# A fused attention, maxout and softplus kernel on one core: the last two blocks of an output phase interleaved by tiles, and loads and preparations moved

## The chip, the core and the metric

The kernel runs on one core of a Trainium2 chip as one program. A core has five engines with one instruction queue each: TensorE (PE) multiplies matrices and writes PSUM; VectorE (DVE), ScalarE (ACT) and GpSimd (POOL) work element by element; SyncE (SP) issues most of the DMA transfers, and ACT issues some. The metric is the device time of one execution in microseconds (us); lower is better.

## The reference

```python
def sm_attn(qq, kk, vv):                       # per batch and head: 8 batches, 8 heads
    s = scale * np.matmul(qq, kk.transpose(0, 1, 3, 2))
    s = s - np.max(s, axis=-1, keepdims=True)
    a = np.exp(s)
    a = a / (np.sum(a, axis=-1, keepdims=True) + 1e-09)
    return np.matmul(a, vv)
p_packed = sm_attn(p, k, v)                    # p: 32 x 64, k and v: 576 x 64
out = sm_attn(q, p_packed, p_packed)           # q: 576 x 64
x = np.ascontiguousarray(attn_out.transpose(0, 2, 1, 3)).reshape(B * S, H * D)   # 4608 x 512
h = np.maximum(np.maximum(x @ w1, x @ w2), x @ w3)         # d_ff 768
x = (h @ w_out).astype(np.float32)
h = x @ w_in                                               # d_ff 2048
g = np.maximum(h, 0.0) + np.log1p(np.exp(-np.abs(h)))      # softplus
return (g @ w_out).astype(np.float32)
```

The weights arrive as 64-bit floats and are narrowed on the chip. Every float32 product is made of three products of rounded halves (hi x hi, hi x lo, lo x hi), so each operand is split into a hi part (a copy by ACT, L125) and a lo part (a subtraction by DVE or POOL, L127).

## The kernel before

The first part goes batch by batch, n = 0 to 7. A hand-written order opens it (batch 0 and what batch 1 needs); batches 1 to 7 are the loop `for n in range(1, B)`. A batch has ten slots. Slots 0 to 5 are the first layer of the first network: each slot has three units (u = 3 * slot + w), a unit is twelve matmuls of 288 columns (`three`, L481), and its PSUM result is copied by ACT for w = 0 (L508) and folded in by DVE with a maximum for w = 1 and 2 (L510, tile m). "m17" below is the DVE maximum of unit 17, the last one of a batch, "m4" that of unit 4. Slots 6 to 9 are the second layer (`layer2`), four times 36 matmuls. Between the units stands the attention of the batch after (`small_work`): its first scores at unit 5 (`scores1`, PE tile ps_s at L286, with transposed k), the transposed weights at units 9 to 12, the values at unit 13 (`values`, L357, with the tile vt), and its second scores directly behind unit 17 (`scores2`, also L286, with transposed q). The weights packed for the first layer are ps_w at L459.

q and k come in four loads of two heads each (g = 0 to 3, `load_raw`, L186), v in one load (`load_v`, L198, tile vt). DVE transposes each q and k load (L253, L256, tile vT). A score takes its heads in the order g = 0 to 3, twice over.

PE's order in this part is pinned (`pinned`), SP's too (`in_turn`). The order on DVE, ACT and POOL is not written down: a scheduler that models the times of instructions and of transfers decides it when the program is built, and on the chip each engine then executes its list in that order.

In the last batch the preparations of the second part stand in the table `BATCH_END`: loads, sums and splits of the first tokens (loadx, sumx, splitx) and of the first weight pairs (load, sum, split).

The second part is written out in order for PE, DVE, ACT and SP. It has five blocks of tokens, c = 0 to 4: four of 2 x 512 tokens and a short one of 2 x 256. For each of eight column pairs j, `layer3` makes seven products of six matmuls (L960, four PSUM buffers of tag l3), adds them up in the tile h (one buffer of tag h; ACT at L977, DVE at L975), and `finish` applies softplus (L998) and splits the result into ghi and glo (two buffers each). `layer4` multiplies these into four accumulators acc0 to acc3, one for each 128 tokens, three matmuls each (L1024, L1025, L1026); the third one needs glo. In the long blocks `second_half` does the same for the kept second halves. `store` copies an accumulator out (ACT for even tiles at L1031, DVE for odd ones at L1033) and issues four DMAs (L1038), in the short block two from SP and two from ACT.

Of the kernel before, what the change touches and what calls it, by code (L numbers as in the profile page):

```python
# [8 lines left out]
F32 = mybir.dt.float32  # L9
# [10 lines left out]
def packed_attention_maxout_softplus(  # L20
# [741 lines left out]
    def narrow_ahead():  # L762
# [19 lines left out]
        4: [("sumx", 2), ("splitx", 2), ("load", 0)],  # L782
        5: [("sumx", 3), ("splitx", 3), ("load", 1)],
        6: [("sum", 0), ("split", 0)],
        7: [("load", 2)],
        8: [("sum", 1), ("split", 1)],
        9: [("load", 3)],
    }

    for n in range(1, B):  # L790
        for slot in range(F1 + KC):
# [4 lines left out]
            if slot < F1:  # L796
                if slot == 1 and n + 1 < B:
                    in_turn(load_v, n + 1)
                for w in range(3):
                    small_work(n, 3 * slot + w)  # L800
                    pinned(layer1_unit, n, slot, w)
            else:
                small_work(n, 2 * F1 + slot)
                pinned(layer2, n, slot - F1)
# [3 lines left out]
            for at, ahead, g, which in loads:  # L808
                if at == slot and n + ahead < B:
                    in_turn(load_raw, n + ahead, g, which)  # L810
            store_narrowed()
            if 0 < n < B - 1 and slot < F1:
# [123 lines left out]

    w2t, kept, hs, gt, accs = {}, {}, {}, {}, {}
    NTT = CH // P
# [24 lines left out]
    def layer3(c, j, aside):  # L963


        def between(at):
            for fn, *args in aside.get(at, ()):
                fn(*args)

        w, wide = pairs.pop(j), BLOCKS[c][1]  # L970
        h = cp.tile([P, 7 * CH], F32, tag="h", name="h")
        h = hs[c, j] = h[:, : 7 * wide].rearrange("p (a t) -> p a t", a=7)

        def plus(o, a, ps):
            add(out=h[:, o], in0=h[:, a], in1=ps, op=ALU.add)  # L975

        nc.scalar.activation(out=h[:, 3], in_=product(c, w, 0, 0), func=AF.Copy)  # L977
        between(0)
        plus(0, 3, product(c, w, 1, 1))
        plus(4, 3, product(c, w, 4, 4))  # L980
        between(1)
        ps = product(c, w, 3, 3)
        plus(5, 4, ps)
        plus(6, 4, product(c, w, 5, 5))
        plus(3, 6, ps)
        between(2)
        plus(2, 6, product(c, w, 2, 6))
        plus(1, 5, product(c, w, 6, 2))
        between(3)

    def split_g(key, src):
        hi = gp.tile([P, CH], F32R, tag="ghi", name="ghi")
        lo = gp.tile([P, CH], F32R, tag="glo", name="glo")
        split(src, hi, lo)
        gt[key] = (hi, lo)

    def softplus(out, x):
        nc.scalar.activation(out=out, in_=x, func=AF.Softplus)  # L998

    def finish(c, j):  # L1000

        h = hs.pop((c, j))
        if BLOCKS[c][1] == CH:
            if j == 0:
                kept[c] = gsp.tile([P, F2, CH], F32, tag="gs", name="gs").rearrange(
                    "p (i j) t -> p i j t", i=2
                )
            softplus(h[:, 0:3:2], h[:, 0:3:2])
            softplus(kept[c][:, :, j], h[:, 1:4:2])
            mine = [h[:, 0], h[:, 2]]  # L1010
        else:
            softplus(h[:, 0:4], h[:, 0:4])
            mine = [h[:, 2 * i : 2 * i + 2].rearrange("p a t -> p (a t)") for i in range(2)]
        for i in range(2):
            split_g((c, j, i), mine[i])

    def layer4(c, half, f, tts, first, last):
        ghi, glo = gt[c, f % FP, f // FP]
        whi, wlo = w2t[f]
        for tt in tts:  # L1020
# [5 lines left out]
            nc.tensor.matmul(ps, glo[:, cols], whi, start=False, stop=last)  # L1026

    def store(c, half, tt, o):
        ps = accs.pop(tt)
        if tt % 2 == 0:  # L1030
            nc.scalar.activation(out=o, in_=ps, func=AF.Copy)  # L1031
# [17 lines left out]
    def second_half(c, aside):  # L1049
        order = [j + FP * i for j in range(FP) for i in range(2)]  # L1050

        def ready(f):
            split_g((c, f % FP, f // FP), kept[c][:, f // FP, f % FP])

        ready(order[0])
        store_first(c)
        for i, f in enumerate(order[:-1]):
# [3 lines left out]
            else:  # L1061
                for tt in range(NTT):
                    layer4(c, 1, f, [tt], False, False)
                    layer4(c, 1, order[-1], [tt], False, True)
            for fn, *args in aside.get(i, ()):
# [19 lines left out]
    with tc.manual_schedule(engines={E.PE, E.DVE, E.Activation, E.SP}):  # L1085
        for f in (0, FP, 1, 1 + FP):
            load_w2(f)
        for i, (c, j) in enumerate(seq):
            aside = {0: [], 1: [], 2: [], 3: []}
            if c == 0:  # L1090
                for m in {0: (), 1: (0,), 2: (1,), 3: (2, 3)}.get(j, (j,)):
# [10 lines left out]
            if c + 1 < NCH:  # L1102
                for part in range(2):
                    if j == (FP - 3 if c == 0 else 1) + part:
                        aside[3].append((load_x2, c + 1, part))
                    if j == FP - 1 and part == 0 or j == FP - 2 and part == 1 and c > 0:
                        aside[0].append((sum_x2, c + 1, part))
            layer3(c, j, aside)
            if i + 2 < len(seq):
                get_pair(*seq[i + 2])  # L1110
            halves = BLOCKS[c][1] == CH
            if j > 0:
                for a in range(2):
                    layer4(c, 0, j - 1 + FP * a, range(NTT), j == 1 and a == 0, False)
            finish(c, j)
            if j == FP - 1:
# [10 lines left out]
                else:  # L1127
                    for tt in range(NTT):
                        for a in range(2):
                            layer4(c, 0, j + FP * a, [tt], False, a == 1)  # L1130
                    store_first(c)
# [36 lines left out]
```

## Time and profile before

| what | us |
|---|---|
| median of 3 runs | 1255.85 (1255.2 to 1256.78) |
| the profiled execution, its own time | 1259.18 |
| its span, first to last instruction | 1257.3 |
| PE busy | 1238.8 (99%) |
| DVE busy | 687.2 (55%) |
| ACT busy | 463.3 (37%) |
| POOL busy | 117.6 (9%) |

The profiled execution took 3.3 us more than the median of the three runs; its own time holds 1.9 us outside its span. Matmuls are pipelined and their ends are modelled, so the distance between the starts of two matmuls says more than PE's busy share. A value in square brackets behind a row is the time that the engine stood idle before that row, and what ended the wait.

### The profile page before, as it was taken

What the parts mean: (1) busy time and instruction counts of PE and PEld (TensorE: products, weight loads), DVE (VectorE), ACT (ScalarE), POOL (GpSimd) and SP (SyncE); (2) the same over time, 40 slices, a digit from 0 to 9 for tenths busy, and PEclk for the clock granted to TensorE, in tenths of its full rate; (3) what the DMA queues carried; (4) which work ended last, traced back from release to release, by engine and by line L of the source; (5) the groups of instructions that cost most, each with busy time, mean ns of one, the idle gap of its engine ahead of it and who ended that gap; (6) DMA issues with size and microseconds to landing.
All of it is one profiled execution on the core that took longest, in us unless ns stands there. A gap on an engine that the chain in (4) does not pass through costs nothing.

```text
span 1257.3 us, 21088 instructions
## 1 busy us (share of the span) xinstructions
PE 1238.8 (99%) x8647; PEld 1060.9 (84%) x8647; DVE 687.2 (55%) x1070; ACT 463.3 (37%) x686; POOL 117.6 (9%) x112
## 2 busy tenths in 40 slices
PE   8899999999999999999999999999999999999998
PEld 6688989898989899888888888888888888888897
DVE  2975757565666649577564444634455354452443
ACT  3744343434343435344342222423224222232222
POOL 1432212222231201000000000000000000000000
PEclk8999999999999999999999999999999999999999
DMA  9878585869596612665523333315334143330541
GB/s 241 260 212 210 143 230 160 212 191 250 155 239 171 175 52 98 232 252 184 192 68 107 137 118 126 117 34 209 117 117 126 25 159 125 126 135 1 200 177 43
DMA packets 87008, 192.55 MB, mean 153 GB/s; under 512 B 12160, under 2 KB 56448, under 8 KB 81792
## 3 DMA queue, kind: packets, MB, share of 16 engines
q1 hardware_dynamic: 81920, 181.24, 47.9%
q10 hardware_dynamic: 4992, 9.96, 2.3%
q8 instruction: 68, 1.11, 0.4%
q14 instruction: 28, 0.23, 0.1%
HBM read 149.23 MB, written 41.94 MB: 152 GB/s over the span
## 4 chain that ended last, share of the span: by engine, by line
PE 92%; DMA 4%; DVE 2%; issue 1%; ACT 0%; SPq 0%; DVEq 0%; ACTq 0%
PE ps L481 28%; PE ps L960 27%; PE acc L1026 11%; PE acc L1025 10%; PE acc L1024 10%; PE ps_w L459 2%; DMA qraw<-in_q_dram 2%; PE ps_s L286 1%; DMA vt<-in_v_dram 1%; PE ps_v L357 1%; PE ps_e L330 1%; DVE x2lo L127 1%; DVE xu L833 0%; DMA praw<-in_p_dram 0%; DVE m L510 0%
## 5 line engine op out<-in xcount | busy, mean ns | idle before, releaser
L960 PE MATMUL ps<-x2hi,wc 128*128 128x512 f32 (+1 forms) x1120 | 322.9, 369 | 1.2 <-ACT h L977 1.2
L975 DVE TENSOR_TENSOR h<-h,ps 128x512 f32<-128x512 f32 (+1 forms) x280 | 173.8, 633 | 114.4 <-PE ps L960 104.5
L960 PEld LDWEIGHTS ps<-x2hi,wc 128*128 128x128 f32 x1120 | 203.6, 188 | 37.2 <-ACT h L977 1.4
L1026 PE MATMUL acc<-w2hi,glo 128*128 128x512 f32 x576 | 225.4, 391 | 0.0
L1025 PE MATMUL acc<-w2lo,ghi 128*128 128x512 f32 x576 | 224.8, 390 | 0.0
L1024 PE MATMUL acc<-w2hi,ghi 128*128 128x512 f32 x576 | 224.5, 390 | 0.0
L960 PE MATMUL ps<-x2lo,wc 128*128 128x512 f32 (+1 forms) x560 | 206.4, 369 | 0.0
L127 DVE TENSOR_TENSOR glo<-h,ghi 128x512 fp32r<-128x512 f32 x80 | 54.8, 692 | 159.9 <-ACT ghi L125 159.9
L1026 PEld LDWEIGHTS acc<-w2hi,glo 128*128 128x128 f32 x576 | 108.1, 188 | 24.6 <-DVE glo L127 2.1
L1024 PEld LDWEIGHTS acc<-w2hi,ghi 128*128 128x128 f32 x576 | 108.2, 188 | 23.7 <-ACT ghi L125 1.2
L998 ACT ACTIVATE h<-h 128x1024 f32<-128x1024 f32 x40 | 42.4, 1060 | 232.0 <-DVE h L975 232.0
L481 PE MATMUL ps<-a2hi,pwhi 128*128 128x288 f32 x576 | 127.8, 303 | 0.0
L1025 PEld LDWEIGHTS acc<-w2lo,ghi 128*128 128x128 f32 x576 | 108.1, 188 | 22.9
L481 PE MATMUL ps<-a2hi,pwlo 128*128 128x288 f32 x576 | 123.2, 295 | 0.4 <-DVE pwlo L127 0.4
L481 PE MATMUL ps<-a2lo,pwhi 128*128 128x288 f32 x576 | 123.3, 296 | 0.0
L960 PEld LDWEIGHTS ps<-x2lo,wc 128*128 128x128 f32 x560 | 105.5, 188 | 18.4
L481 PEld LDWEIGHTS ps<-a2hi,pwhi 128*128 128x128 f32 x576 | 91.8, 189 | 15.1 <-ACT m L508 5.0
L510 DVE TENSOR_TENSOR m<-ps,m 128x576 f32<-128x576 f32 x96 | 72.4, 754 | 49.9 <-PE ps L481 45.1
L481 PEld LDWEIGHTS ps<-a2hi,pwlo 128*128 128x128 f32 x576 | 92.7, 189 | 0.7 <-DVE pwlo L127 0.7
L481 PEld LDWEIGHTS ps<-a2lo,pwhi 128*128 128x128 f32 x576 | 92.8, 189 | 0.0
L127 DVE TENSOR_TENSOR pwlo<-ps_w,pwhi 128x1024 fp32r<-128x1024 f32 (+1 forms) x40 | 44.5, 1114 | 84.0 <-ACT pwhi L125 83.9
L127 DVE TENSOR_TENSOR glo<-gs,ghi 128x512 fp32r<-128x512 f32 x64 | 44.1, 690 | 78.7 <-ACT ghi L125 70.6
(103 smaller groups left out, 1486.7 us busy)
## 6 DMA issues: line engine op xcount, KB each, us to landing
wc<-wic SPq DMA_DIRECT2D x32, 1792.0 KB
qraw<-in_q_dram SPq DMA_DIRECT2D x112, 140.0 KB
wic<-wc SPq DMA_DIRECT2D x8, 1792.0 KB
kraw<-in_k_dram SPq DMA_DIRECT2D x96, 140.0 KB
vt<-in_v_dram SPq DMA_DIRECT2D x8, 1152.0 KB
wraw<-in_moe_w_dram SPq DMA_DIRECT2D x18, 512.0 KB
x2d<-xs ACTq DMA_DIRECT2D x32, 288.0 KB
xu<-x2d SPq DMA_DIRECT2D x72, 128.0 KB
```

What stands on the lines that cost most here:

```text
L127: engine.tensor_tensor(out=lo, in0=src, in1=hi.bitcast(F32), op=ALU.subtract)
L286: nc.tensor.matmul(ps[G][cols, hh, :HS], w[rows, cols], x[rows, g, hh * HS : hh * HS + HS], start=True, stop=True,)
L330: nc.tensor.transpose(ps[: 32 * TI, i // hi, (i % hi) * P : (i % hi) * P + P], e[:, i], ident,)
L459: nc.tensor.matmul(ps[cols, G, : units * P].rearrange("p (w x) -> p w x", w=units), ppT[n][rows, cols], wsb[rows, 4 * c : 4 * c + units, g ...
L481: nc.tensor.matmul(o, w, xx, start=first, stop=last)
L510: nc.vector.tensor_tensor(out=m, in0=ps[:, :, :HS], in1=ms[n, f], op=ALU.max)
L960: nc.tensor.matmul(out, l, r, start=(i == 0), stop=(i == len(terms) - 1))
L975: add(out=h[:, o], in0=h[:, a], in1=ps, op=ALU.add)
L998: nc.scalar.activation(out=out, in_=x, func=AF.Softplus)
L1024: nc.tensor.matmul(ps, ghi[:, cols], whi, start=first, stop=False)
L1025: nc.tensor.matmul(ps, ghi[:, cols], wlo, start=False, stop=False)
L1026: nc.tensor.matmul(ps, glo[:, cols], whi, start=False, stop=last)
```

## The change

- `last_two` replaces the order of the last two blocks f of an output phase. Before, each tile tt took its three matmuls of the first block and then its three of the second. Now the first block goes over tiles 0, 1 and 2, then the second over 0 and 1, then the first over 3, then the second over 2 and 3. It is used at the end of `second_half` and at the end of the short block.
- In the short block two pairs j share one tile h, each in its half, in place of a new tile each; and the softplus and the splits of pair 0 are issued in three steps between the products of pair 1.
- The last tile of the whole kernel is copied out in two halves, one by ACT and one by DVE.
- `load_v` of the next batch moves from the start of slot 1 to slot 0, behind the first of the three q loads there. SP then issues v ahead of the q loads g = 1 and 2.
- In `BATCH_END` sumx 3, splitx 3 and load 1 go from slot 5 to slot 6, sum 0 and split 0 to slot 7, split 1 to slot 9.

What these do to the order on the engines is shown at three places. First, DVE at the end of the first layer in batch 3. In the names, vT_3162 is the transposed q of batch 4, qraw_3164 its last load (g = 3), m_3426 to m_3507 the maxima of units 13, 14, 16 and 17, x32 the narrowing of later weights, s2 the second scores. Before:

```order
L510 TENSOR_TENSOR m_3426<-ps_1_3413,m_3338 128x576
L510 TENSOR_TENSOR m_3441<-ps_1_3428,m_3426 128x576
L253 STREAM_TRANSPOSE vT_3162<-qraw_3164 128x576
L111 SCALAR_TENSOR_TENSOR x32_3315<-x32_3315,raw64_3068 128x512
L510 TENSOR_TENSOR m_3492<-ps_1_3479,m_3473 128x576
L111 SCALAR_TENSOR_TENSOR x32_3450<-x32_3450,raw64_3174 128x512
L510 TENSOR_TENSOR m_3507<-ps_1_3494,m_3492 128x576
L111 SCALAR_TENSOR_TENSOR x32_3525<-x32_3525,raw64_3231 128x512
L397 STREAM_TRANSPOSE s2_3553<-ps_s_3535 128x576
```

The last transpose of q stood behind unit 14, and the other three ahead of these rows. The same stretch now (qraw_3056, qraw_3061 and qraw_3164 are the loads g = 1, 2 and 3):

```order
L510 TENSOR_TENSOR m_3426<-ps_1_3413,m_3338 128x576
L253 STREAM_TRANSPOSE vT_3162<-qraw_3056 128x576
L510 TENSOR_TENSOR m_3441<-ps_1_3428,m_3426 128x576
L510 TENSOR_TENSOR m_3492<-ps_1_3479,m_3473 128x576
L510 TENSOR_TENSOR m_3507<-ps_1_3494,m_3492 128x576
L253 STREAM_TRANSPOSE vT_3162<-qraw_3061 128x576
L253 STREAM_TRANSPOSE vT_3162<-qraw_3164 128x576
L111 SCALAR_TENSOR_TENSOR x32_3315<-x32_3315,raw64_3070 128x512
L397 STREAM_TRANSPOSE s2_3553<-ps_s_3535 128x576
```

The transposes of g = 2 and g = 3 have moved behind the maximum of unit 17. It is so in batches 3, 4 and 5; in batches 1, 2 and 6 one transpose of q (g = 3) stands behind it. PE's order in this part is the same before and after.

Second, DVE at units 1 to 5 of batch 3, where kraw_2735 is the last load of the k that the first scores at unit 5 use. Before:

```order
L510 TENSOR_TENSOR m_3047<-ps_1_3034,m_3025 128x576
L256 STREAM_TRANSPOSE vT_2979<-kraw_2735 128x6x3x32
L510 TENSOR_TENSOR m_3104<-ps_1_3091,m_3089 128x576
L111 SCALAR_TENSOR_TENSOR x32_3170<-x32_3170,raw64_2670 128x512
L127 TENSOR_TENSOR pwlo_3107<-ps_w_3108,pwhi_3106 128x1024
```

The transpose stood ahead of m_3104, the maximum of unit 4. Now:

```order
L510 TENSOR_TENSOR m_3047<-ps_1_3034,m_3025 128x576
L510 TENSOR_TENSOR m_3104<-ps_1_3091,m_3089 128x576
L256 STREAM_TRANSPOSE vT_2979<-kraw_2735 128x6x3x32
L127 TENSOR_TENSOR pwlo_3107<-ps_w_3108,pwhi_3106 128x1024
L111 SCALAR_TENSOR_TENSOR x32_3170<-x32_3170,raw64_2670 128x512
```

It stands behind unit 4, in batches 3 to 6. In batch 1 it stood there before, and does now; in batch 2 it stands ahead in both.

Third, ACT at the very end, where ho is the output tile of the short block. Before:

```order
L1031 ACTIVATE ho_12033<-acc0_11418 128x512
L1038 DMA out_0_dram<-ho_12033 32x512 x4
L1031 ACTIVATE ho_12033<-acc2_11426 128x512
L1038 DMA out_0_dram<-ho_12033 32x512 x4
```

Now, with the copy of half a tile among the DMA issues:

```order
L1046 ACTIVATE ho_12026<-acc0_11417 128x512
L1053 DMA out_0_dram<-ho_12026 32x512 x4
L1046 ACTIVATE ho_12026<-acc2_11425 128x512
L1053 DMA out_0_dram<-ho_12026 32x512 x2
L1043 ACTIVATE ho_12026<-acc3_11429 128x256
L1053 DMA out_0_dram<-ho_12026 32x512 x2
```

The half copy of acc3 stands behind the copy of acc2 and its two DMA issues. The diff:

```diff
@@ -780,11 +780,10 @@
         2: [("splitx", 0), ("loadx", 2)],
         3: [("sumx", 1), ("splitx", 1), ("loadx", 3)],
         4: [("sumx", 2), ("splitx", 2), ("load", 0)],
-        5: [("sumx", 3), ("splitx", 3), ("load", 1)],
-        6: [("sum", 0), ("split", 0)],
-        7: [("load", 2)],
-        8: [("sum", 1), ("split", 1)],
-        9: [("load", 3)],
+        6: [("sumx", 3), ("splitx", 3), ("load", 1)],
+        7: [("sum", 0), ("split", 0), ("load", 2)],
+        8: [("sum", 1)],
+        9: [("split", 1), ("load", 3)],
     }
 
     for n in range(1, B):
@@ -794,8 +793,6 @@
                 layer1_split(n, slot - 1)
                 l1_done = last_of(mybir.EngineType.Activation)
             if slot < F1:
-                if slot == 1 and n + 1 < B:
-                    in_turn(load_v, n + 1)
                 for w in range(3):
                     small_work(n, 3 * slot + w)
                     pinned(layer1_unit, n, slot, w)
@@ -808,6 +805,8 @@
             for at, ahead, g, which in loads:
                 if at == slot and n + ahead < B:
                     in_turn(load_raw, n + ahead, g, which)
+                    if (slot, g) == (0, 0):
+                        in_turn(load_v, n + 1)
             store_narrowed()
             if 0 < n < B - 1 and slot < F1:
                 narrow_ahead()
@@ -968,8 +967,10 @@
                 fn(*args)
 
         w, wide = pairs.pop(j), BLOCKS[c][1]
-        h = cp.tile([P, 7 * CH], F32, tag="h", name="h")
-        h = hs[c, j] = h[:, : 7 * wide].rearrange("p (a t) -> p a t", a=7)
+        if wide == CH or j == 0:
+            room[0] = cp.tile([P, 7 * CH], F32, tag="h", name="h")
+        at = (7 * wide * j) % (7 * CH)
+        h = hs[c, j] = room[0][:, at : at + 7 * wide].rearrange("p (a t) -> p a t", a=7)
 
         def plus(o, a, ps):
             add(out=h[:, o], in0=h[:, a], in1=ps, op=ALU.add)
@@ -988,16 +989,16 @@
         plus(1, 5, product(c, w, 6, 2))
         between(3)
 
-    def split_g(key, src):
+    def split_g_steps(key, src):
         hi = gp.tile([P, CH], F32R, tag="ghi", name="ghi")
         lo = gp.tile([P, CH], F32R, tag="glo", name="glo")
-        split(src, hi, lo)
         gt[key] = (hi, lo)
+        return split_steps(src, hi, lo)
 
     def softplus(out, x):
         nc.scalar.activation(out=out, in_=x, func=AF.Softplus)
 
-    def finish(c, j):
+    def finish_steps(c, j):
 
         h = hs.pop((c, j))
         if BLOCKS[c][1] == CH:
@@ -1011,8 +1012,14 @@
         else:
             softplus(h[:, 0:4], h[:, 0:4])
             mine = [h[:, 2 * i : 2 * i + 2].rearrange("p a t -> p (a t)") for i in range(2)]
-        for i in range(2):
-            split_g((c, j, i), mine[i])
+        yield
+        halves = [split_g_steps((c, j, i), mine[i]) for i in range(2)]
+        if j == 0 and BLOCKS[c][1] < CH:
+            for steps in halves:
+                next(steps)
+            yield
+        for steps in halves:
+            every(steps)
 
     def layer4(c, half, f, tts, first, last):
         ghi, glo = gt[c, f % FP, f // FP]
@@ -1025,9 +1032,17 @@
             nc.tensor.matmul(ps, ghi[:, cols], wlo, start=False, stop=False)
             nc.tensor.matmul(ps, glo[:, cols], whi, start=False, stop=last)
 
+    def last_two(c, half, f0, f1):
+
+        for tts, last in (([0, 1, 2], 0), ([0, 1], 1), ([3], 0), ([2, 3], 1)):
+            layer4(c, half, (f0, f1)[last], tts, False, last == 1)
+
     def store(c, half, tt, o):
         ps = accs.pop(tt)
-        if tt % 2 == 0:
+        if c == NCH - 1 and tt == NTT - 1:
+            nc.scalar.activation(out=o[:, : DM // 2], in_=ps[:, : DM // 2], func=AF.Copy)
+            nc.vector.tensor_copy(o[:, DM // 2 :], ps[:, DM // 2 :])
+        elif tt % 2 == 0:
             nc.scalar.activation(out=o, in_=ps, func=AF.Copy)
         else:
             nc.vector.tensor_copy(o, ps)
@@ -1050,7 +1065,7 @@
         order = [j + FP * i for j in range(FP) for i in range(2)]
 
         def ready(f):
-            split_g((c, f % FP, f // FP), kept[c][:, f // FP, f % FP])
+            every(split_g_steps((c, f % FP, f // FP), kept[c][:, f // FP, f % FP]))
 
         ready(order[0])
         store_first(c)
@@ -1059,9 +1074,7 @@
             if i < F2 - 2:
                 layer4(c, 1, f, range(NTT), i == 0, False)
             else:
-                for tt in range(NTT):
-                    layer4(c, 1, f, [tt], False, False)
-                    layer4(c, 1, order[-1], [tt], False, True)
+                last_two(c, 1, f, order[-1])
             for fn, *args in aside.get(i, ()):
                 fn(*args)
         if BLOCKS[c + 1][1] < CH:
@@ -1087,6 +1100,7 @@
             load_w2(f)
         for i, (c, j) in enumerate(seq):
             aside = {0: [], 1: [], 2: [], 3: []}
+            halves = BLOCKS[c][1] == CH
             if c == 0:
                 for m in {0: (), 1: (0,), 2: (1,), 3: (2, 3)}.get(j, (j,)):
                     for f in (m, m + FP):
@@ -1105,14 +1119,19 @@
                         aside[3].append((load_x2, c + 1, part))
                     if j == FP - 1 and part == 0 or j == FP - 2 and part == 1 and c > 0:
                         aside[0].append((sum_x2, c + 1, part))
+            if j == 1 and not halves:
+                for at in range(3):
+                    aside[at].append((next, late, None))
             layer3(c, j, aside)
             if i + 2 < len(seq):
                 get_pair(*seq[i + 2])
-            halves = BLOCKS[c][1] == CH
             if j > 0:
                 for a in range(2):
                     layer4(c, 0, j - 1 + FP * a, range(NTT), j == 1 and a == 0, False)
-            finish(c, j)
+            if j == 0 and not halves:
+                late = finish_steps(c, j)
+            else:
+                every(finish_steps(c, j))
             if j == FP - 1:
                 if halves:
                     for a in range(2):
@@ -1125,9 +1144,7 @@
                             at.setdefault(2 * part + 3, []).append((sum_x2, c + 1, part + 2))
                     second_half(c, at)
                 else:
-                    for tt in range(NTT):
-                        for a in range(2):
-                            layer4(c, 0, j + FP * a, [tt], False, a == 1)
+                    last_two(c, 0, j, j + FP)
                     store_first(c)
 
 
```

## Rows read from the trace of the kernel before

**Rows 1.** The page, busy us, share of the span and instructions.

```profile
PE 1238.8 (99%) x8647; PEld 1060.9 (84%) x8647; DVE 687.2 (55%) x1070; ACT 463.3 (37%) x686; POOL 117.6 (9%) x112
```

**Rows 2.** Timeline of PE, batch 3: start, us, engine, line, output<-inputs, count.

```profile
249.54 1.55 PE L357 MATMUL ps_v<-vt,e1T 96*32 96x64 f32 x96 [0.57 <-DMA vt<-in_v_dram]
...
259.29 1.20 PE L286 MATMUL ps_s<-vT,ppT 64*32 64x288 f32 x32
260.28 1.06 PE L459 MATMUL ps_w<-wsb,ppT 64*32 64x512 f32 x16
```

**Rows 3.** Timeline of DVE, batch 3, units 14 to 17 and the end.

```profile
254.50 0.76 DVE L510 TENSOR_TENSOR m<-ps,m 128x576 f32<-128x576 f32 x1 [0.77 <-PE ps L481]
255.17 0.77 DVE L253 STREAM_TRANSPOSE vT<-qraw 128x576 f32<-128x576 f32 x1
...
259.39 0.76 DVE L510 TENSOR_TENSOR m<-ps,m 128x576 f32<-128x576 f32 x1
...
273.94 1.42 DVE L127 TENSOR_TENSOR a2lo<-a,a2hi 128x576 fp32r<-128x576 f32 x2
```

**Rows 4.** Timeline of PE, batch 1, first scores behind unit 4.

```profile
113.08 1.09 PE L459 MATMUL ps_w<-wsb,ppT 64*32 64x512 f32 x16
...
114.93 1.19 PE L286 MATMUL ps_s<-vT,pT 64*32 64x288 f32 x28 [0.32 <-DVE vT L256]
116.05 0.53 PE L481 MATMUL ps<-a2hi,pwhi 128*128 128x288 f32 x2
```

**Rows 5.** Timeline of DVE, batch 1, the last transpose of k.

```profile
113.93 0.95 DVE L256 STREAM_TRANSPOSE vT<-kraw 128x576 f32<-128x576 f32 x1
```

**Rows 6.** Timeline of PE, batch 4, first scores behind unit 4.

```profile
289.94 1.09 PE L459 MATMUL ps_w<-wsb,ppT 64*32 64x512 f32 x16
...
291.93 0.53 PE L481 MATMUL ps<-a2hi,pwhi 128*128 128x288 f32 x2
```

**Rows 7.** Chain that ended last, in batch 3: start, us, what.

```profile
261.35 20.97 PE ps L481 x156
```

**Rows 8.** Stretches: length, busy PE, PEld, DVE, ACT, POOL, granted clock, DMA, GB/s.

```profile
36.40:39.80 3.40, 1.04 (x10) 0.80 (x8) 3.40 (x5) 2.07 (x5) 2.79 (x3) 1.00 0.45 147
39.80:43.20 3.40, 3.30 (x37) 1.87 (x38) 3.40 (x5) 1.88 (x4) 2.54 (x3) 0.50 0.54 171
...
78.00:82.00 4.00, 2.43 (x102) 1.90 (x100) 2.86 (x7) 1.58 (x3) 0.00 (x0) 1.00 0.60 150
```

**Rows 9.** Timeline of PE at 39.9 us.

```profile
39.90 2.17 PE L286 MATMUL ps_s<-vT,pT 64*32 64x288 f32 x32 [2.46 <-ACT pT L268]
```

**Rows 10.** Timeline of DVE, end of batch 7.

```profile
493.98 0.75 DVE L127 TENSOR_TENSOR hlo<-m,hhi 128x576 fp32r<-128x576 f32 x1
```

**Rows 11.** Timeline of ACT, end of batch 7.

```profile
493.09 0.69 ACT L125 ACTIVATE hhi<-m 128x576 fp32r<-128x576 f32 x1 [2.15 <-DVE m L510]
```

**Rows 12.** Waits of PE's weight loads: us in total, times, longest us.

```profile
PEld acc L1026 <- DVE glo L127: 2.1, 5, 0.4
```

**Rows 13.** Timeline of PE, short block: pair 1, then the last two blocks.

```profile
1176.22 0.39 PE L960 MATMUL ps<-x2hi,wc 128*128 128x256 f32 x1 [1.20 <-ACT h L977]
...
1247.03 0.39 PE L1024 MATMUL acc<-w2hi,ghi 128*128 128x512 f32 x1
...
1247.71 0.48 PE L1024 MATMUL acc<-w2hi,ghi 128*128 128x512 f32 x1
...
1248.76 0.39 PE L1024 MATMUL acc<-w2hi,ghi 128*128 128x512 f32 x1
```

**Rows 14.** Timeline of ACT and its queue, short block.

```profile
1237.95 0.38 ACT L977 ACTIVATE h<-ps 128x256 f32<-128x256 f32 x1 [0.82 <-DVE glo L127]
...
1248.96 0.60 ACT L1031 ACTIVATE ho<-acc 128x512 f32<-128x512 f32 x1 [1.32 <-PE acc L1026]
1249.59 0.87 ACTq L1038 DMA_DIRECT2D out_dram<-ho  x2
```

**Rows 15.** Timeline of DVE, the last copy.

```profile
1253.07 0.69 DVE L1033 COPY ho<-acc 128x512 f32<-128x512 f32 x1 [2.03 <-PE acc L1026]
```

More of the change, by code (lines that the diff above doesn't have):

```diff
@@ L935, in packed_attention_maxout_softplus @@
     acc = ctx.enter_context(tc.tile_pool(name="acc", bufs=1, space=PSUM, reuse_waits="tile"))
-    w2t, kept, hs, gt, accs = {}, {}, {}, {}, {}
+    w2t, kept, hs, gt, accs, room = {}, {}, {}, {}, {}, {}
     NTT = CH // P
```

## The prediction

> **What bounds the kernel now.** I read the page first, then the waits of PE and of its weight loads, then PE's timeline at each wait, and beside it DVE's and ACT's. PE is busy 1238.8 of 1257.3 us [rows 1]; the other engines have a third of the span or more to spare. So an edit can give back only what PE still stands idle, and it can cost whatever new wait it puts in front of PE. The reader should see two things in the timelines. The waits that the change aims at are short: 0.57 us for v in batch 3 [rows 2], 1.20 us in the short block [rows 13], five of at most 0.4 us before the last block of an output phase [rows 12]. And in batches 1 to 7 PE's scores need all four transposes by DVE, so where these stand in DVE's list is as good as PE's own order.
>
> **What the change gives back.** In the profiled execution's own time:
>
> Value loads: v is issued ahead of two q loads, so the 0.57 us [rows 2] go: -0.6. In the other batches PE shows no such wait, so nothing more is to be had there, and 0 is the other end.
>
> Batch 7: DVE's lo part began at 493.98 [rows 10], with part of a sum ahead of it, though its hi part ended at 493.78 [rows 11]. With the sums moved behind it, it begins at once: -0.2. All sums and splits of pairs 0 and 1 come one slot later; they are covered by the layer-2 matmuls of slots 6 to 9, and I count them at nothing (up to +1 if the cover is gone).
>
> `last_two`: three matmuls take 1247.71 - 1247.03 = 0.68 us, the next three, which wait for glo, 1248.76 - 1247.71 = 1.05 [rows 13], so 0.37 is lost. There are five such waits [rows 12]; the four in the long blocks give 4 x 0.37 = -1.5. Now nine matmuls (2.0 us) stand between, more than the 0.4 that is missing.
>
> Short block, pairs 0 and 1: PE waits 1.20 us for the tile h [rows 13], and with a half each it need not: -1.2. What is late next is the split of pair 0, which ACT and DVE now do between products of pair 1. PE asks for its lo part after 42 matmuls of 0.12 us plus two of 0.23, 5.5 us after pair 0; softplus, splits and sums ahead of it end a little sooner by my count, so nothing to +0.3.
>
> **The tail.** Its own wait of 0.37 goes too, yet the end moves back. ACT's list decides: copy of acc0, four DMA issues, copy of acc2, two issues, half copy of acc3, two issues. Copies take 0.60, a half 0.38, a pair of issues 0.87 [rows 14]. A copy began 0.20 after the start of the matmul that follows its tile (1248.96 after 1248.76 [rows 13, 14]). Counting from 1247.03 in steps of 0.227: tile 0 is done after twelve matmuls, so its copy runs 1249.96 to 1250.56, two pairs of issues to 1252.33, copy of acc2 to 1252.98, its pair to 1253.87, the half to 1254.30. Before, the last copy ended at 1253.76 [rows 15], and everything behind it is alike. So +0.5. The nearest other ends are -0.7 (issues that hold nothing up) and +1.0.
>
> On this the Trainium skill has a rule (DMA: Bandwidth & Descriptors, section "Issuing engines are not separate DMA queues"): issuing from several engines saves only the sequencer's time of issuing, which is usually small. Here a pair of issues is longer than the copy beside it [rows 14], and they stand in one list with it, so the trace decides; by the rule the tail would be -0.7 and the sum 1.2 less.
>
> **What the moved load does to DVE.** Modelled arrivals of q g = 1, 2 and 3 come later, and the built order shows the transposes of q behind m17: one in batches 1, 2 and 6, two in batches 3, 4 and 5. The queue is in order, m17 cannot begin before unit 17 has left PE, and PE's very next work is the second scores. Let T be the start of these scores, 259.29; their 32 records (16 matmuls in two passes) took 0.99, 0.031 each, until ps_w at 260.28 [rows 2]. m17 began at T + 0.10; a transpose began 0.67 after the maximum ahead of it and took 0.77 [rows 3]. So the first transpose ends at T + 1.54, a second 0.67 later at T + 2.21. How PE takes such a wait is shown by batch 1, where a transpose of k stood behind m4: it ended at 114.88 [rows 5], PE went on at 114.93, and the 28 records left took 1.12, 0.040 each [rows 4]. The head g = 3 is first asked for by record 13, which leaves 20, or 0.80. One transpose: ps_w at T + 1.59 + 0.80 = T + 2.39 instead of T + 0.99, +1.40. Two: T + 3.06, +2.07. Together 3 x 1.40 + 3 x 2.07 = +10.4.
>
> First scores: in batches 3 to 6 the transpose of k g = 3 now stands behind m4. Batch 1 has that order already: 2.97 us from ps_w to the next unit [rows 4] against 1.99 in batch 4 [rows 6], so 0.98 lost. There the wait came after 4 records; here it comes after 12, which hides 8 x 0.031 = 0.25. Four times 0.73: +2.9 (0.5 to 0.98 each).
>
> Behind the scores DVE's chain to a2lo shifts with PE and takes one x32 more. It ended at 275.36 [rows 3], and unit 0 of the next batch follows 144 of 156 matmuls, at 261.35 + 19.36 = 280.7 [rows 7], so 5 us of cover; gone, each us past it would be paid in six batches. SP's k loads g = 1 to 3 queue behind the store of x32_3315, which comes some 6 us later; their transposes stand a batch end away, so I count nothing.
>
> **The clock.** After PE had stood 2.46 us [rows 9] and been busy 1.04 of 3.40, the granted clock was 0.50 (1.2 GHz) for the next 3.4 us; where it was busy 2.43 of 4.00 the clock stayed at 1.00 (2.4 GHz) [rows 8]. A wait for two transposes leaves PE idle from T + 0.25 to T + 1.59 and from T + 1.71 to T + 2.26, 1.9 us, so some 1.5 busy in 3.4: between the two rows. A wait for one idles 1.2, nearer to the second row. A stretch of 3.4 us at half the clock costs 1.7. Of the three longer waits I let half fall: 1.5 x 1.7 = +2.6, with 0 and 5.1 as ends.
>
> The Trainium skill (TensorE: Matmul & The Clock Gate, section "HAM oscillation — how this bites in real kernels") warns of idle gaps of PE only above a length that no wait here reaches. But the gap of 2.46 us [rows 9] lies below that length too, and the clock fell behind it, so I let the row weigh more.
>
> **Sum.** -0.6 - 0.2 - 1.5 - 1.2 + 0.5 + 10.4 + 2.9 + 2.6 = +12.9: a span of 1270.2, an execution of 1272.1 in place of 1259.18. The profiled execution was 3.3 above the median of the runs; on the median it is 1255.85 + 12.9 = 1268.8.
>
> **Rivals.** (1) The clock holds through every wait: all terms but the last, 1266.2. This is also what the skill's rule on gaps would give. For it, the short matmuls that run inside the wait; against it, the stretch at 39.8.
> (2) The waits are absorbed: PE's scores do stall, but PE would have stood later in the same batch, or the transposes end before they are asked for. Then only the gains are left, 1255.85 - 3.0 = 1252.9, faster. It decides once less than 3.0 of the 13.3 us of new waits are left. For it, DVE is busy only 687.2 of 1257.3 us [rows 1]; against it, the order on DVE is fixed and PE has no later wait in a batch that could take it up, bar the 0.57.
> (3) The clock falls at all six second scores: 1255.85 + 10.3 + 6 x 1.7 = 1276.4. Against it, the shorter waits are near the row that held.
> (4) q itself lands too late behind v: two us more in each of six batches on top of the forecast, 1280.8. Against it, the last q load stood behind v before too, and its transpose at 255.17 waited for nothing [rows 3].
>
> **How the numbers follow.** Forecast 0.55, rivals 0.27, 0.07, 0.07 and 0.04. The range 1262.5 to 1272.5 takes in the forecast with none to three falls, rival 1, the k term at its lower end and the tail at either; it leaves out rivals 2 to 4, 0.15, and a little of the rest. Under 0.2% (2.5 us) a measurement of this kernel can't tell from no change. Rival 2 is faster, 0.07; between lies almost nothing, 0.01; the rest is slower, 0.92.
>
> **What would show it.** In the profile after: PE waits on DVE vT (L253) of 1 to 2 us in second scores of batches 1 to 6, and on L256 of about half a us in first scores of batches 3 to 6; a batch longer by 2 to 4 us; stretches of granted clock 0.50 behind some of the waits. No wait for v in batch 3, none for glo before the last block, none for h at pair 1. The half copy of acc3 ends later than acc3's DVE half by over 1 us. The forecast is wrong if PE shows no wait of a us at the second scores, or if the clock is 1.00 throughout and the time still above 1270.

## The result, and the profile after

The changed kernel takes 1269.92 us (median of six runs, 1267.47 to 1272.9), the kernel before 1256.16 (six runs): a ratio of 1.011 with a 95% interval of 1.0095 to 1.0125. So it is 13.8 us slower. The forecast was 1268.8, +12.9, and slower with a chance of 0.92.

The profiled executions have spans of 1257.3 and 1271.1, also 13.8 apart. The second part of the kernel shows where to look first. PE's rows there, of the kernel before, its first product and its last matmul (start, us, engine, line, output<-inputs):

```profile
509.82 0.39 PE L960 MATMUL ps<-x2hi,wc 128*128 128x512 f32 x1
...
1252.64 0.39 PE L1026 MATMUL acc<-w2hi,glo 128*128 128x512 f32 x1
```

And of the changed kernel:

```profile
525.77 0.39 PE L959 MATMUL ps<-x2hi,wc 128*128 128x512 f32 x1
...
1265.16 0.39 PE L1033 MATMUL acc<-w2hi,glo 128*128 128x512 f32 x1
```

From the first product to the last matmul it went from 742.82 to 739.39, 3.4 us less: the part that the change rewrote most did get faster. But it begins 15.95 us later, and behind the last matmul 5.94 us follow in place of 4.66. So the loss lies ahead of the second part, but for 1.3 us of tail: in the attention part, where the change moved one load and, in the last batch, some preparations.

The page's first line, to be held beside [rows 1]:

```profile
PE 1248.6 (98%) x8647; PEld 1067.0 (84%) x8647; DVE 681.9 (54%) x1070; ACT 463.2 (36%) x687; POOL 116.8 (9%) x112
```

It tells next to nothing: as many matmuls, and PE's share falls by one point. The waits of PE and of its weight loads (PEld) tell it (us in total, times, longest us):

```profile
PE ps_s L286 <- DVE vT L253: 5.8, 6, 1.3
...
PE ps_s L286 <- DVE vT L256: 1.6, 5, 0.3
...
PEld ps_s L286 <- DVE vT L253: 10.5, 9, 1.8
...
PEld ps_s L286 <- DVE vT L256: 4.3, 5, 0.9
```

Scores now wait for DVE's transposes of q (L253) at six second scores, nine transposes in all, and for those of k (L256) at five first scores. Before, there was one such wait, the one of batch 1 [rows 4]. The waits for glo [rows 12], for the tile h [rows 13] and for v in batch 3 [rows 2] have left the list.

The second scores of batch 4, before, on PE's timeline:

```profile
317.72 1.20 PE L286 MATMUL ps_s<-vT,ppT 64*32 64x288 f32 x32
318.71 1.06 PE L459 MATMUL ps_w<-wsb,ppT 64*32 64x512 f32 x16
319.71 0.40 PE L481 MATMUL ps<-hhi,wo_hi 128*128 128x288 f32 x1
```

After:

```profile
326.42 0.69 PE L286 MATMUL ps_s<-vT,ppT 64*32 64x288 f32 x8
328.03 1.58 PE L286 MATMUL ps_s<-vT,ppT 64*32 64x288 f32 x22 [0.91 <-DVE vT L253]
329.21 0.63 PE L459 MATMUL ps_w<-wsb,ppT 64*32 64x512 f32 x6
329.44 0.41 PE L286 MATMUL ps_s<-vT,ppT 64*32 64x288 f32 x2
329.64 1.07 PE L459 MATMUL ps_w<-wsb,ppT 64*32 64x512 f32 x10
330.63 0.53 PE L481 MATMUL ps<-hhi,wo_hi 128*128 128x288 f32 x2
```

And DVE's timeline beside it, the maximum of unit 17 and the two transposes behind it:

```profile
326.53 0.76 DVE L510 TENSOR_TENSOR m<-ps,m 128x576 f32<-128x576 f32 x1 [0.77 <-PE ps L481]
327.21 1.43 DVE L253 STREAM_TRANSPOSE vT<-qraw 128x576 f32<-128x576 f32 x2
```

From the scores' start to the next unit, behind ps_w, it was 319.71 - 317.72 = 1.99; now it is 330.63 - 326.42 = 4.21, +2.22. With T for the scores' start, the transposes begin at T + 0.79 and end at T + 2.22. It is so in batches 3, 4 and 5.

The first scores of batch 4, after, on PE; before it was 1.99 from ps_w to the next unit [rows 6]:

```profile
297.65 1.09 PE L459 MATMUL ps_w<-wsb,ppT 64*32 64x512 f32 x16
298.53 0.68 PE L286 MATMUL ps_s<-vT,pT 64*32 64x288 f32 x12
299.53 1.16 PE L286 MATMUL ps_s<-vT,pT 64*32 64x288 f32 x20 [0.32 <-DVE vT L256]
300.62 0.53 PE L481 MATMUL ps<-a2hi,pwhi 128*128 128x288 f32 x2
```

Now 2.97: +0.98, the whole loss that batch 1 had shown [rows 4].

In batch 1 a single transpose stands behind the maximum, and yet it cost more than in batch 2. DVE there:

```profile
142.42 0.69 DVE L111 SCALAR_TENSOR_TENSOR x<-x,raw 128x512 int32<-128x512 int32 x1 [2.34 <-POOL raw L95]
143.03 1.61 DVE L510 TENSOR_TENSOR m<-ps,m 128x576 f32<-128x576 f32 x2
144.56 0.77 DVE L253 STREAM_TRANSPOSE vT<-qraw 128x576 f32<-128x576 f32 x1
```

A narrowing (L111) that itself waited for POOL came ahead of the maxima of units 16 and 17, so the transpose began 1.15 behind the scores' start of 143.41, not 0.79.

The clock, in stretches as in [rows 8]:

```profile
78.00:82.00 4.00, 2.06 (x99) 1.56 (x97) 2.29 (x7) 1.37 (x3) 0.00 (x0) 1.00 0.70 184
82.10:85.50 3.40, 3.22 (x21) 1.56 (x22) 1.42 (x3) 1.15 (x2) 0.00 (x0) 0.50 0.72 199
...
326.42:329.82 3.40, 2.49 (x47) 1.02 (x48) 2.10 (x3) 2.43 (x4) 1.65 (x2) 1.00 0.01 2
329.82:333.22 3.40, 3.40 (x34) 2.59 (x20) 2.93 (x5) 1.03 (x1) 3.16 (x4) 1.00 0.36 112
```

Behind all six of the new waits at second scores the granted clock stayed at 1.00 (2.4 GHz); the last two rows are batch 4. Up to the last matmul the record has 0.50 (1.2 GHz) at two places only: near 41, where it was so before too [rows 8], and at 82.1, behind waits of PE of 1.17 and 0.68 us at batch 0's values and just after them.

The tail, ACT and its queue:

```profile
1262.87 0.60 ACT L1046 ACTIVATE ho<-acc 128x512 f32<-128x512 f32 x1 [2.31 <-PE acc L1033]
1263.49 1.81 ACTq L1053 DMA_DIRECT2D out_dram<-ho  x4
1265.35 0.60 ACT L1046 ACTIVATE ho<-acc 128x512 f32<-128x512 f32 x1 [1.89 <-DMA out_dram<-ho]
1265.98 0.85 ACTq L1053 DMA_DIRECT2D out_dram<-ho  x2
1266.88 0.38 ACT L1043 ACTIVATE ho<-acc 128x256 f32<-128x256 f32 x1 [0.93 <-ACT ho L1046]
1267.75 0.85 ACTq L1053 DMA_DIRECT2D out_dram<-ho  x2
```

And DVE's half of the last tile:

```profile
1267.29 0.42 DVE L1044 COPY ho<-acc 128x256 f32<-128x256 f32 x1 [3.05 <-ACT ho L1043]
```

The copies and issues come in the order forecast: the half copy of acc3 stands behind two copies and six issues on ACT. What was not forecast is DVE's half: it waited 3.05 us for ACT's half, so the two do not run side by side. The sign named for this place (ACT's half ends over 1 us behind DVE's) did not come: DVE's half ended 0.45 behind ACT's.

### The profile page after: what moved, and what is told of

Its sections match the earlier page's. It is cut to its first block, busy times and chain, and to the rows that moved or that the text cites. A ratio compares the mean times of both kernels' runs of the same rounds, so it can differ in the third digit from the quotient of the medians.

```text
span 1271.1 us, 21070 instructions
## 1 busy us (share of the span) xinstructions
PE 1248.6 (98%) x8647; PEld 1067.0 (84%) x8647; DVE 681.9 (54%) x1070; ACT 463.2 (36%) x687; POOL 116.8 (9%) x112
## 4 chain that ended last, share of the span: by engine, by line
PE 91%; DVE 4%; DMA 2%; issue 1%; ACT 1%; SPq 1%; POOL 0%; ACTq 0%; DVEq 0%; POOLq 0%
PE ps L959 27%; PE ps L481 26%; PE acc L1033 10%; PE acc L1032 10%; PE acc L1031 10%; PE ps_w L459 2%; PE ps_s L286 1%; PE ps_e L330 1%; PE ps_k L231 1%; DVE m L510 1%; DMA qraw<-in_q_dram 1%; PE ps_v L357 1%; DVE x2lo L127 1%; DVE xu L832 0%; DVE vT L256 0%
```

## The experiments

Times are medians. Each stands against the kernel before, timed beside it: 1256.27 (29 runs) for the load put back, the load alone, both orders fixed and the last tile whole; 1256.45 (35 runs) for the other four.

**The load put back.** The one edit, in the loop over slots:

```diff
+                if slot == 1 and n + 1 < B:
+                    in_turn(load_v, n + 1)
                 for w in range(3):
...
                     in_turn(load_raw, n + ahead, g, which)
-                    if (slot, g) == (0, 0):
-                        in_turn(load_v, n + 1)
```

> The changed kernel with the value load back at the start of slot 1; all else of the change stays. DVE's list in batches 1 to 7 is then as before. Theory A (the order on DVE is what costs): the nine waits of PE on transposes in batches 1 to 6 go, and what is left is what the second part gained in the two traces: its first product to its last matmul 742.82 before, 739.39 now, -3.4; its tail 4.66 before and 5.94 now, +1.3; some -0.2 at the end of batch 7. So 2.3 us below the kernel before, 1253.9. Theory B (the moved sums and splits of the last batch, or the shared tile, have a part in the loss): 1258 or more, with waits of PE left in batches 1 to 7.

1254.66; ratio to before 0.9989 (0.9975 to 1.0003). PE's weight loads wait for a transpose of DVE only where they did before, once, in batch 1:

```profile
PEld ps_s L286 <- DVE vT L256: 0.9, 1, 0.9
```

So 15.3 us of the changed kernel's time hang on this one edit, and the rest of the change is worth about -1.6, with an interval that just touches no change. Theory B falls.

**The load alone moved.** The same edit the other way round, on the kernel before.

> The kernel before with the one edit that v is issued behind the first q load of slot 0. Theory A: DVE's list in batches 1 to 6 becomes that of the changed kernel, so the whole loss comes: 2.22 us in each of batches 3 to 5 and 1.56 to 1.93 in 1, 2 and 6 at the second scores, 0.98 in batches 3 to 6 at the first scores, less 0.6 of the wait for v: 14.9 us, so 1271. Theory B (part of the loss belongs to the other edits): under 1268.

1272.52 (four runs), ratio 1.0125 (1.0101 to 1.0149): +16.2, a little above the 14.9 worked out, which lies within the interval. The waits are those of the changed kernel:

```profile
PE ps_s L286 <- DVE vT L253: 5.7, 6, 1.2
...
PE ps_s L286 <- DVE vT L256: 1.6, 5, 0.3
```

With the first experiment this shows that the load's place is enough for the loss, and needed for it.

**The load early, DVE's order fixed.** Is it the order, or data that lands later?

```diff
+            t = turned.get((n + 1, {(1, 1): "k", (F1 - 1, 1): "q"}.get((f, w))))
+            with tc.issue_after(t) if t else nullcontext():
-            nc.vector.tensor_tensor(out=m, in0=ps[:, :, :HS], in1=ms[n, f], op=ALU.max)
+                nc.vector.tensor_tensor(out=m, in0=ps[:, :, :HS], in1=ms[n, f], op=ALU.max)
...
                     transpose_kq(n + ahead, g, which)
+                    turned[n + ahead, which] = last_of(mybir.EngineType.DVE)
```

> The changed kernel with the value load early, but the order on DVE fixed: the maximum of unit 16 is put behind all transposes of q of its batch, the maximum of unit 4 behind all transposes of k. Theory A (order alone; the data is there in time): no wait of PE on a transpose in batches 2 to 6 (batch 1 keeps its first-score wait of 1.0), v without a wait, so 0.6 below the kernel with the load back, 1253.3. Theory C (q itself lands later behind v, and the late place in the list was needed): DVE waits for qraw ahead of the maxima of units 14 to 17, PE waits for its buffers, 5 us or more slower than A, 1258 or above.

1254.88, ratio 0.999 (0.9978 to 1.0003): all of the loss is gone, with v still issued early. DVE in batch 3, with the transposes of q between the maxima of units 14 and 16:

```profile
254.34 0.76 DVE L514 TENSOR_TENSOR m<-ps,m 128x576 f32<-128x576 f32 x1
255.01 1.43 DVE L255 STREAM_TRANSPOSE vT<-qraw 128x576 f32<-128x576 f32 x2
257.71 0.76 DVE L514 TENSOR_TENSOR m<-ps,m 128x576 f32<-128x576 f32 x1 [1.27 <-PE ps L483]
```

The transposes waited for nothing and DVE then stood idle for 1.27 us: q was there, and DVE had the time. In no batch from 1 to 6 does a transpose of q or k wait for its load in this trace. The order was late, not the data. Theory C falls. The 0.6 expected from v is not to be seen in the medians (1254.88 and 1254.66).

**Only q fixed.** As above, without the entry for k.

> The changed kernel with the transposes of q alone fixed ahead of the maximum of unit 16; those of k stay behind the maximum of unit 4 in batches 3 to 6. Theory: the waits of the second scores go, 1.93 + 2 x 1.56 + 3 x 2.22 = 11.7 us by the traces, and 4 x 0.98 = 3.9 at the first scores stay, so 3.9 above the kernel with both fixed (1254.9): 1258.8. Rival (the two waits are one: the late k follows from DVE's late chain behind the second scores, and goes with it on the chip): 1255.

1258.09, 3.2 above the kernel with both fixed (timed apart, each beside the kernel before: ratios 1.0016 and 0.999). PE's waits on q are gone from the list, those on k are all there:

```profile
PE ps_s L288 <- DVE vT L258: 1.6, 5, 0.3
```

So the two waits are separate, and by the medians q costs some 12 us and k some 3 (by the traces 11.7 and 3.9). The intervals of the two kernels, 0.9999 to 1.0034 and 0.9978 to 1.0003, still overlap a little, so the 3 for k rests on the five waits in the trace as well.

**The last tile whole.** The value load back, and `store` without the branch for the last tile:

```diff
-        if c == NCH - 1 and tt == NTT - 1:
-            nc.scalar.activation(out=o[:, : DM // 2], in_=ps[:, : DM // 2], func=AF.Copy)
-            nc.vector.tensor_copy(o[:, DM // 2 :], ps[:, DM // 2 :])
-        elif tt % 2 == 0:
+        if tt % 2 == 0:
```

> The value load back in slot 1, and the last tile copied whole by DVE as before. In the changed kernel's trace DVE's half copy started 3.05 us late, behind ACT's half copy, which stood behind the copy of acc2 and a pair of issues. Theory A (the half copy on ACT's list sets the end): the last pair of issues on ACT begins when the pair for acc2 ends, 1.67 us behind the last matmul instead of 2.59, so the end comes 0.9 us earlier than with the value load back alone. Rival: DVE's wait is only for the other half and the issues rule anyway: 0.4 or less.

1253.59, ratio 0.998 (0.9963 to 0.9997); 1.07 below the kernel with the load back alone. Its trace shows less: 1250.1 - 1244.48 = 5.62 us behind the last matmul, in place of 1252.7 - 1246.69 = 6.01. ACT's last issues did end as expected:

```profile
1244.67 0.60 ACT L1043 ACTIVATE ho<-acc 128x512 f32<-128x512 f32 x1 [1.89 <-DMA out_dram<-ho]
1245.30 1.79 ACTq L1050 DMA_DIRECT2D out_dram<-ho  x4
```

That is 2.61 behind the last matmul, in place of 3.45, but only 0.4 of these 0.84 reached the end of the span. So by the traces the half copy costs 0.4, what the rival gave, not the 0.9 of theory A. The medians can't decide it: the two kernels' intervals overlap, and 1.07 is within the noise.

**The old table for the last batch.** On the kernel with the load back and the last tile whole, `BATCH_END` as it was.

> As the kernel with the load back and the last tile whole, and the table of the last batch's preparations as before as well. Theory: the sums and splits are covered by PE in either place; only the wait for hlo at the end of the first layer of batch 7 comes back to 0.42 from 0.26, so +0.2, which the timing can't show (1253.8). Rival: the later places matter, for good or ill, by a us or more: PE waits at another place of batch 7 or at the first products.

1254.45, ratio 0.9981 (0.9962 to 0.9999). Its trace has the wait for hlo at 0.42 again, and 1246.79 - 507.40 = 739.39 from first product to last matmul, as in the changed kernel. The moved preparations are worth nothing that can be measured.

**The old order of tiles.**

```diff
-        for tts, last in (([0, 1, 2], 0), ([0, 1], 1), ([3], 0), ([2, 3], 1)):
-            layer4(c, half, (f0, f1)[last], tts, False, last == 1)
+        for tt in range(NTT):
+            layer4(c, half, f0, [tt], False, False)
+            layer4(c, half, f1, [tt], False, True)
```

> As the kernel with the load back and the last tile whole, but with the last two blocks of each output phase in the old order of tiles. Theory: five waits for glo of 0.37 come back, +1.8 at the last matmul, but the accumulators are then finished one after the other, and the tail behind the last matmul is 4.7 again (trace of before) instead of 5.6: +0.9 net, 1254.5. Rival: the waits come back and the tail stays: +1.8, 1255.4.

1255.19, ratio 0.9996 (0.9979 to 1.0013): 1.6 above the same kernel with `last_two`, but the two intervals overlap, so what follows goes by the traces. The five waits are back:

```profile
PEld acc L1033 <- DVE glo L127: 2.1, 5, 0.4
```

From the first product to the last matmul it takes 1249.00 - 507.71 = 741.29, against 1244.48 - 505.13 = 739.35: 1.9 more. The tail is 1253.7 - 1249.00 = 4.70 against 5.62. So by the traces `last_two` gives 1.9 and loses 0.9 of it at the end, since it finishes tiles 0 and 1 later and leaves the same issues to follow; that nets 1.0, near the theory's 0.9 and not the rival's 1.8. What is left of the second part's 3.4, about 1.5, belongs to the shared tile of the short block, with its splits in steps. This trace shows it apart: with the old order of tiles in both, the short block takes 1249.00 - 1164.79 = 84.21 us from its first product to the last matmul here and 1252.64 - 1166.95 = 85.69 in the kernel before.

**The parts that pay, together.** The load back, the last tile whole, tile 2 of the short block copied by DVE too, and batch 1's old wait on k taken away:

```diff
-        if tt % 2 == 0:
+        if tt % 2 == 0 and not (c == NCH - 1 and tt == 2):
...
         transpose_kq(2, g, "k")
+        if g == 1:
+            dve = (i for i in reversed(nc.cur_bb.bb.instructions) if i.engine == mybir.EngineType.DVE)
+            last_k = next(dve)
...
+            with tc.issue_after(last_k) if (n, f, w) == (1, 1, 1) else nullcontext():
```

> Three edits on the changed kernel: the value load back in slot 1; the last three tiles of the short block copied by DVE, whole, so that ACT copies only acc0 and then issues; and in batch 1 the maximum of unit 4 put behind the last transpose of k. Theory: against the kernel with the load back and the last tile whole (1253.6 median) PE no longer waits 0.98 us in batch 1, and ACT's list has one copy of 0.60 less ahead of its last issues, so they end 0.6 earlier: 1.6 less, 1252.0, and 4 us below the kernel before. Rival: the last issues are held up by SP's list of eight, not by ACT's copies, and another part of the opening takes up the 0.98: 1253.6.

1252.38, ratio 0.9963 (0.9945 to 0.9981): 4.1 below the kernel before, and the lowest median of all. Its interval lies below no change, though its near end just within 0.2%, and it overlaps those of the kernels with the next two medians (1253.59 and 1254.45). PE's first scores of batch 1 run through:

```profile
109.46 1.09 PE L459 MATMUL ps_w<-wsb,ppT 64*32 64x512 f32 x16
110.34 1.18 PE L286 MATMUL ps_s<-vT,pT 64*32 64x288 f32 x32
111.45 0.53 PE L481 MATMUL ps<-a2hi,pwhi 128*128 128x288 f32 x2
```

1.99, against 2.97 [rows 4]. ACT's tail is one copy and eight issues:

```profile
1241.40 0.60 ACT L1047 ACTIVATE ho<-acc 128x512 f32<-128x512 f32 x1 [2.31 <-PE acc L1037]
1242.03 4.09 ACTq L1054 DMA_DIRECT2D out_dram<-ho  x8
```

They end 1246.12 - 1243.69 = 2.43 behind the last matmul, and the span 5.11 behind it, 0.5 less than with tile 2 on ACT. The issues themselves end only 0.18 earlier (2.43 against 2.61), not the 0.6 expected: ACT copies once less, but here the issues alone fill its queue.

## Why the prediction was right, and where its terms were off

The mechanism held: the moved load put transposes behind maxima on DVE, and PE's scores waited for them. The sum held too, +13.8 measured and +12.9 forecast, but in part by luck: the forecast has 2.6 for a clock that did not fall, and its other terms were too small by 2.4. Term by term, by the traces (the tail's +0.5 of the forecast held the fifth wait of `last_two`, -0.4, which stands by itself here):

| term | forecast | measured |
|---|---|---|
| second scores, six batches | +10.4 | 1.93 + 2 x 1.56 + 3 x 2.22 = +11.7 |
| first scores, batches 3 to 6 | +2.9 | 4 x 0.98 = +3.9 |
| clock behind these waits | +2.6 | 0 |
| `last_two`, five waits | -1.5 - 0.4 | -1.9 |
| shared tile | -1.2 | -1.5 |
| v, hlo | -0.8 | -0.8 |
| tail behind the last matmul | +0.9 (0.5 + 0.4) | +1.3 |
| sum | +12.9 | +12.7 |

**The waits.** DVE's side came to the hundredth (T + 2.21 forecast, T + 2.22 measured). PE's side was 0.15 too small in each batch: from PE's start behind the transpose to the next unit it took 1.95 in batch 2 (205.35 to 207.30), not the 1.80 that 0.80 and 1.0 make. Batch 1 added 0.37 by the narrowing ahead of its maxima, a wait of DVE for POOL that I had not looked for. PE itself stood idle 0.85 to 1.26 us at these scores, over a us in batch 1 alone, while the next unit came 1.56 to 2.22 later.

At the first scores the 0.25 that twelve records in place of four should hide were not hidden: what is left behind the wait took 1.09 for 20 records, and 1.12 for 28 in batch 1. The step at fault is the price per record (0.031 and 0.040). The starts of the single matmuls in the traces show why: score matmuls begin in groups of up to eight at once, and from one group to the next it takes 0.24 to 0.27 us, whether a group has two or eight. Behind the wait, batch 4 has groups of 8, 8, 2 and 2 (after; they begin at 299.53, 299.80, 300.04 and 300.28), batch 1 of 8, 8, 6 and 6 (before; at 114.93, 115.20, 115.44 and 115.68). These are four each, as many as the 32 records take without a wait, so the records that ran ahead of it saved nothing.

**The clock.** This step failed: "Of the three longer waits I let half fall". None did, in this trace or in that of the load alone, twelve waits in all. I took PE for idle 1.9 us in such a stretch, but the trace has 0.91: the eight records ahead of the wait take 0.69 in it, and those between the two transposes fill the time to the second. PE was busy 2.49 of 3.40, a larger part than the 2.43 of 4.00 at which the clock had held [rows 8]. Rival 1 was right on the clock. Of the 3.7 between its 1266.2 and the measured time, 2.4 are the terms that were too small, 0.3 is the kernel before itself (1255.85 in three runs, 1256.16 in six), and some 1.0 stands in no term. The prediction also called itself wrong if the clock held throughout and the time was still above 1270: behind the waits it held, and 1269.92 is only just below.

**The rest of the difference.** Batch 0 and the opening are 1.6 longer in the trace after than in that of before. In the trace after, PE waited 1.17 us at batch 0's values, and the clock fell behind it. SP's order of loads up to there is the same in both kernels, so I take it for scatter of that stretch: batch 0's second scores begin at 88.07 in the trace of before, at 89.65 in that of after, and between 84.47 and 86.84 in the five traces with the load put back. Against chance, the four traces with the load early have it at 88.17 to 91.59, later than all six others. The same fall of the clock stands in the traces of both kernels with the load early and DVE's order fixed, and not in that of the load alone, nor in any with the load late. Whether the early load has a part in it stays open; with the order fixed it cost nothing that the medians show. The trace of before has 0.5 at the values of batch 6 that the trace after lacks, a wait for nothing that the profile shows (two others with the load late have 0.27 and 0.71 there). These two, +1.6 and -0.5, are what the 13.8 between the spans has more than the table's 12.7.

**The tail.** The order on ACT was as forecast and the end came 0.4 later still, mostly because DVE's half waited for ACT's. Four issues took 1.81 us on ACT, and the copy of acc2 stood behind them. The Trainium skill (DMA: Bandwidth & Descriptors, section "Issuing engines are not separate DMA queues") calls the time that a sequencer spends on issuing usually small relative to the DMA itself. In this tail that is not what counted: the issues stood in one list with ACT's copies, and their 1.81 us were three times the 0.60 of the copy behind them.

**Rivals 2 to 4.** The waits were not absorbed, the clock fell at none of the six second scores, and q was in time: with the order fixed, DVE's transposes wait for nothing.

## What to carry to other kernels

Where a scheduler orders an engine's list by modelled arrivals, moving one load can move work on an engine that the edit does not name; compare the built lists before the times, and look for what now stands behind an instruction that itself waits for the bottleneck. If the load is wanted early, fix the order with an edge; here that took back the whole loss. Where matmuls run in groups, price a wait by the groups left behind it and not by the matmuls. A gain at PE in the last phase is worth only what the stores behind it let through: here half of what `last_two` gave came back as a longer tail.

## What the runs showed of the hardware that I had not expected

Two copies of the halves of one accumulator, one by ACT and one by DVE, into different columns of one tile, ran one after the other in the program as built: DVE's waited 3.05 us and began 0.03 after ACT's ended (1267.29, after 1266.88 + 0.38). The row names ACT's half as what it waited for; why the program has it wait, the trace does not tell.

Score matmuls that a wait cut off took as long for 20 records (1.09 us) as for 28 (1.12): both are four groups of up to eight that begin together, 0.24 to 0.27 us apart.

The clock fell after PE's 2.46 us of idleness in the opening [rows 9], and at 82.1 after a stretch in which PE was busy 2.06 of 4.00 us, but not after six waits of 0.85 to 1.26 us with 2.14 to 2.55 busy of 3.40. The place in the opening is in all ten traces: in the six where PE waited 2.43 to 2.47 us there the clock fell, in the four where it waited 1.17 to 1.70 it did not.
